# Later token chunks of a GeGLU feed-forward: the gate and up corrections as seven block products with sums outside PSUM

## The chip, the core and the metric

One NeuronCore of a Trainium2 chip runs the whole program. Its engines work side by side, each on its own queue in order: TensorE (PE; its weight loads are shown as PEld), VectorE (DVE), ScalarE (ACT), GpSimd (POOL) and SyncE (SP), which issues most DMAs. Matrix products go to PSUM, eight banks of 128 x 512 float32; operands come from SBUF. Engines wait for each other by semaphores. The metric is the time of one execution on the device in microseconds (us), the median of several.

## The reference

One transformer block in float32 with 2048 tokens of width 640: attention in a window of 256, then a feed-forward of width 1536 with a gate.

```python
def _B_ref(x, w_gate, w_up, w_down):
    return (_gelu(x @ w_gate) * (x @ w_up)) @ w_down

x = A_x
h = x + _A_ref(_layernorm(x, axis=-1), A_wqkv, A_wo)
h2 = h + _B_ref(_layernorm(h, axis=-1), B_w_gate, B_w_up, B_w_down)
return h2
```

## The kernel before

TensorE works in float16 at a quarter of the price of float32, so each float32 operand is split into two float16 parts, a high one and a low one (`wh`, `wl` of a weight; `hh`, `hl` of the normalised tokens). A product is then three matmuls: high x high, high x low, low x high (`parts`). Weights are scaled by a power of two first, so that the low parts don't vanish; `WE` is that exponent, `ffk` holds the factors that undo it.

The feed-forward runs over four chunks of 512 tokens (`NCH`, `CB` blocks of 128) and, in each, over three groups of 512 features (`FG`) of four tiles of 128 (`FT`). For a chunk `c` and a group `fg`, `gate_up` makes for each tile `ft` the gate product and the up product: 5 slices of the width (`KC`) x 3 parts = 15 matmuls of 512 columns into one of two `mm` banks each. `gate_out` then runs beside it: ScalarE takes the gate bank through GELU into `gel`, VectorE multiplies the up bank onto it (`gel`), ScalarE writes the high part `ah`, VectorE the low part `al`. `down` multiplies `ah`, `al` by the down weights: eight groups (4 token blocks x 2 halves of the width) of 12 matmuls of 320 columns, each into an `mm` bank, which VectorE adds to the rows `ht` (`down_out`); that addition frees the bank. Rows that are complete leave for `out_dram`; the next chunk but one then loads its rows into their place (`chunk_lane`), and `norm_lane` normalises them: VectorE's statistics (`BN_STATS`), `lxn`, ScalarE's high part `sph`, VectorE's low part `spl`, and DMA transposes into `hTh`, `hTl`.

The order of instructions on each engine is not written out: the program is a set of lanes (Python generators), and a planner (`Clock`, and the loop at the end of `block_kernel`) keeps a running estimate of each engine's time and takes the next step of the first lane that can start. What it decides while the program is built is fixed on the chip. TensorE's own lane in the feed-forward is `feed_forward`: `gate_up` of a group, then `down` of the group before. Chunk 0 begins while the attention still runs; `split_lane` makes the parts of the weights as they arrive, the high part on ScalarE, the low one on VectorE (`low`; its other branch, ScalarE and GpSimd, is there but unused). All instructions are recorded through one helper, so the profile gives line 190 to all.

```python
for w in (wg_, wu_):
    wh, wl = w.hl
    ps = yield from products(KC, lambda k: parts((wh[:, k, fs], wl[:, k, fs]),
                                                 (hh[:, k, :], hl[:, k, :])),
                             lambda k: k in w.have)
```

Of the kernel before, what the change touches and what calls it, by code (L numbers as in the profile page):

```python
# [11 lines left out]
F32 = mybir.dt.float32  # L12
# [4 lines left out]
ALU = mybir.AluOpType  # L17
# [20 lines left out]


WE = 14  # L40
XE = 10
QE = -23
VE = -20
ME = 15
UE = -43


def _pow2(e):
    return float(2.0 ** e)
# [192 lines left out]
def block_kernel(ctx: ExitStack, tc: tile.TileContext, x, wqkv, wo, wg, wu, wd, out):  # L242
# [21 lines left out]
    def done(name):  # L264
        opened[name] -= 1
# [64 lines left out]
    class Weight:  # L330
# [3 lines left out]
        hl = None  # L334
        loaded = scaled = known = sliced = down = begun = False

        def __init__(self, src, shape, col):
            self.src, self.shape, self.col = src, shape, col
            self.have = set()
            self.raw = {}  # L340

# [24 lines left out]
        def scale(self, lane, tp="tp"):  # L366
            n = self.shape[0]
            am = nc.tile(lnp, [P, 8], F32, "am" + lane, 2 if lane == "0" else 1)
            nc.vector.memset(am[:, n:n + 1], _pow2(-100))
            for i in range(n):  # L370
                if self.hl:

                    yield on("scalar", self.raw[0, i])
                    nc.scalar.activation(self.hl[0][:, i, :], self.raw[0, i], AF.Abs,
                                         accum_out=am[:, i:i + 1])
                    continue
                yield on("vector", when=lambda: (0, i) in self.raw)
# [9 lines left out]
            nc.vector.tensor_scalar(dg, ident, am[:, 7:8], _pow2(-WE), op0=ALU.mult, op1=ALU.mult)  # L387
# [16 lines left out]
            nc.vector.tensor_scalar(pc, pc, _pow2(WE), None, op0=ALU.mult)  # L404
            self.known = True

        def room(self, pool):
# [31 lines left out]
        W[n] = Weight(wqkv[g], [KC, D], C_Q + g)  # L439
    W["o", 0] = Weight(wo, [KC, D], C_WO)  # L440
    for g in range(FG):
        W["g", g] = Weight(wg[g], [KC, 512], C_G + g)
        W["u", g] = Weight(wu[g], [KC, 512], C_U + g)
        W["d", g] = Weight(wd[g], [FT, D], C_D + g)


# [97 lines left out]

    def ff_scales(fg):
        gs, us = C_G + fg, C_U + fg
        nc.vector.tensor_scalar(ffk[:, fg, 0:1], pw[:, gs:gs + 1], _pow2(-WE - XE), None,
                                op0=ALU.mult)
        nc.vector.tensor_scalar(ffk[:, fg, 4:5], pw[:, gs:gs + 1], 0.5 * _pow2(-WE - XE), None,
                                op0=ALU.mult)  # L550
        nc.vector.tensor_scalar(ffk[:, fg, 1:2], sw[:, gs:gs + 1], _pow2(UE), None, op0=ALU.mult)
        nc.vector.tensor_tensor(ffk[:, fg, 3:4], pw[:, us:us + 1], pw[:, gs:gs + 1], op=ALU.mult)

    def ff_scales_down(fg):
        ds_ = C_D + fg
        nc.vector.tensor_scalar(ffk[:, fg, 2:3], ffk[:, fg, 3:4], pw[:, ds_:ds_ + 1],
                                _pow2(-WE - XE - UE - WE - WE), op0=ALU.mult, op1=ALU.mult)


    attn = ExitStack()  # L560
# [480 lines left out]
    def gate_out(c, fg, ft, pss):  # L1041

        pool = ffpools[(c * FG + fg) % 2]
        ah, al = ga[c, fg]
        gel = nc.tile(pool, [P, CB * P], F32, "gel", 2)
# [12 lines left out]
    def gate_up(c, fg):  # L1058
        pool = ffpools[(c * FG + fg) % 2]
        wg_, wu_ = W["g", fg], W["u", fg]  # L1060
        yield pe(when=lambda: wg_.hl and chunk[c] == CB)
        hh, hl = hT[c]
        ah = nc.tile(pool, [P, FT, CB * P], F16, "ah")
        al = nc.tile(pool, [P, FT, CB * P], F16, "al")
        ga[c, fg] = ah, al
        for ft in range(FT):
            fs = slice(ft * P, (ft + 1) * P)
            yield pe(when=lambda: opened["gel"] < 2)
            pss = []
            for w in (wg_, wu_):  # L1070
                yield pe(when=lambda: w.hl)
# [8 lines left out]
                yield  # L1080

    def down(c, fg):
        w = W["d", fg]
# [36 lines left out]
            hts[c].append(ht)  # L1120

    def chunk_lane(c):
        yield ("sync",), need(when=lambda: c == 0 or W["u", 2].ready
                              and (c < 2 or chunk["out", c - 2] == CB), eng="sync")
        load_h(c, ffpools[c % 2], CB)
        if c:
            hT[c] = tuple(nc.tile(ffp, [P, KC, CB * P], F16, n, 2) for n in ("hTh", "hTl"))
            side.extend((LATE, norm_lane(c, bs, n)) for bs, n in (((0, 2), "h"), ((1, 3), "i")))

    def norm_lane(c, bs, lane):  # L1130
        for b in bs:
            yield from layernorm(hts[c][b], lane, *hpart(c, b),
                                 xn=lambda: nc.tile(ffp, [P, D], F32, "lxn", 2), dma=True)
            chunk[c] += 1

    def first_norm_lane():

# [118 lines left out]

    def feed_forward():
        order = [(c, fg) for c in range(NCH) for fg in range(FG)]
        prev = None
        for c, fg in order[1:]:  # L1260
            yield from gate_up(c, fg)
            if prev:
                yield from down(*prev)
            prev = (c, fg)
        yield from down(*prev)

# [140 lines left out]
```

## Time and profile before

| | before |
|---|---|
| median of 3 runs | 1069.77 us (1068.78 to 1072.12) |
| span of the profiled execution, first to last instruction | 1063.8 us |
| PE busy | 1038.2 us, 98% of the span |
| DVE busy | 659.2 us, 62% |
| ACT busy | 461.0 us, 43% |
| POOL busy | 183.4 us, 17% |
| mean granted TensorE clock | 0.995 |

The profiled execution has no time of its own but its span; the median of the runs is 5.97 us above that span. The attention takes some 620 us of it, and from about 697 us on TensorE works on chunks 1 to 3 of the feed-forward. In the profile's rows a group reads: line, engine, operation, output <- inputs with their shapes, count, duration (mean, or min/median/max, in ns). A timeline row begins with start and duration in us; in brackets stands the idle time of the engine just before, and what ended it.

### The profile page before, as it was taken

How to read it: one execution, taken by the hardware profiler on the slowest of the kernel's cores; microseconds unless marked ns; L12 is line 12 of the kernel's file. 1: busy time of each engine (PE TensorE's matmuls, PEld its weight loads, DVE VectorE, ACT ScalarE, POOL GpSimd, SP SyncE). 2: the span in 40 equal slices, each digit the busy share in tenths (PEclk: the TensorE clock that was granted, in tenths of full speed). 3: DMA queues.
4: the chain of work that ended last, by engine and by line, in shares of the span. 5: the costliest groups of instructions: out<-in, count | busy, mean ns of one | idle time of the engine just before them, and what ended most of it. 6: DMA issues, size and time to landing. Idle time of an engine off the chain costs nothing.

```text
span 1063.8 us, 25769 instructions
## 1 busy us (share of the span) xinstructions
PE 1038.2 (98%) x10486; PEld 649.8 (61%) x10486; DVE 659.2 (62%) x1966; ACT 461.0 (43%) x890; POOL 183.4 (17%) x297
## 2 busy tenths in 40 slices
PE   7999899999999999999999999999999999999998
PEld 7977466766776666676655664555545545545546
DVE  5678899997778877677789469823622262322223
ACT  5521666665666656567666835310211120111010
POOL 5000223232233223323332400000000000000000
PEclk9999999999999999999999999999999999999999
DMA  7562444543141321414321034202300040001001
GB/s 285 136 156 69 123 139 106 154 114 78 44 110 57 87 67 52 101 52 94 106 104 51 27 121 153 45 6 99 50 1 1 28 107 15 1 1 50 1 1 50
DMA packets 79382, 80.89 MB, mean 76 GB/s; under 512 B 22240, under 2 KB 58336, under 8 KB 78304
## 3 DMA queue, kind: packets, MB, share of 16 engines
q1 hardware_dynamic: 56160, 68.50, 22.7%
q10 hardware_dynamic: 23104, 10.75, 3.8%
q8 instruction: 82, 1.34, 0.5%
q14 instruction: 36, 0.29, 0.1%
HBM read 54.07 MB, written 20.97 MB: 71 GB/s over the span
## 4 chain that ended last, share of the span: by engine, by line
PE 86%; DVE 8%; DMA 2%; issue 2%; ACT 1%; POOL 0%; SPq 0%; DVEq 0%; ACTq 0%; POOLq 0%
PE mm L190 65%; PE pv L190 9%; PE ra L190 4%; PE rb L190 4%; PE tp L190 4%; DVE junk L190 3%; DMA qk<-qks 1%; DMA kT<-qk 1%; ACT pt L190 1%; DVE gu L190 0%; DVE am L190 0%; DVE lstx L190 0%; DVE w3l L190 0%; DVE ht L190 0%; DMA xt<-in_x_dram 0%
## 5 line engine op out<-in xcount | busy, mean ns | idle before, releaser
L190 POOL TENSOR_SCALAR_AFFINE_SELECT pt<-pt 128x512 f32<-128x512 f32 x240 | 151.0, 651 | 332.6 <-ACT pt L190 327.5
L190 DVE CUSTOM_DVE_ANT_0 junk<-ra,mask 128x384 bf16<-128x384 f32 (+2 forms) x266 | 141.3, 531 | 42.4 <-PE ra L190 21.8
L190 ACT ACTIVATE pt<-rb,esc 128x384 f32<-128x384 f32 (+2 forms) x248 | 131.4, 581 | 67.2 <-PE rb L190 47.1
L190 DVE CUSTOM_DVE_ANT_0 junk<-rb,mask 128x384 bf16<-128x384 f32 (+2 forms) x246 | 130.1, 529 | 42.8 <-PE rb L190 25.7
L190 ACT ACTIVATE pt<-ra,esc 128x384 f32<-128x384 f32 (+2 forms) x232 | 121.8, 577 | 77.0 <-PE ra L190 67.1
L190 DVE SCALAR_TENSOR_TENSOR gel<-mm,ffk,gel 128x512 f32<-128x512 f32 x48 | 36.0, 749 | 146.3 <-PE mm L190 146.3
L190 ACT ACTIVATE gel<-mm,ffk 128x512 f32<-128x512 f32 x48 | 33.0, 688 | 190.6 <-PE mm L190 190.6
L190 PE MATMUL pv<-pt,v 128*21 128x128 f32 x2880 | 105.6, 277 | 0.8 <-ACT oT L190 0.6
L190 DVE SCALAR_TENSOR_TENSOR ht<-mm,ffk,ht 128x320 f32<-128x320 f32 x96 | 52.8, 550 | 80.5 <-PE mm L190 80.3
L190 PEld LDWEIGHTS <-ah 128*128 128x128 f16 x768 | 75.1, 98 | 31.2 <-issue 0.8
L190 ACT CAST ah<-gel 128x512 f16<-128x512 f32 x48 | 29.7, 618 | 128.7 <-DVE gel L190 128.7
L190 PEld LDWEIGHTS pv<-pt,v 128*21 128x21 f32 x2880 | 69.0, 101 | 16.0 <-issue 2.2
L190 PEld LDWEIGHTS <-gu 128*128 128x128 f16 x480 | 45.7, 98 | 53.7 <-issue 1.9
L190 PE MATMUL mm<-hTh,gu 128*128 128x512 f16 x240 | 71.9, 379 | 0.0
L190 PEld LDWEIGHTS <-kT 62*128 62x128 f16 x1440 | 58.3, 95 | 21.4 <-issue 10.9
L190 PEld LDWEIGHTS <-qT 60*128 60x128 f16 x640 | 24.8, 93 | 63.2 <-issue 59.8
L190 PE MATMUL mm<-xl,w1h 128*128 128x256 f16 x200 | 54.7, 273 | 0.0
L190 PE MATMUL mm<-xl,w0h 128*128 128x256 f16 x200 | 54.6, 273 | 0.0
L190 PE MATMUL mm<-xh,w1l 128*128 128x256 f16 x200 | 54.6, 273 | 0.0
L190 PE MATMUL mm<-xh,w1h 128*128 128x256 f16 x200 | 54.6, 273 | 0.0
L190 PE MATMUL mm<-xh,w0l 128*128 128x256 f16 x200 | 54.6, 273 | 0.0
L190 PE MATMUL mm<-xh,w0h 128*128 128x256 f16 x200 | 54.6, 273 | 0.0
(219 smaller groups left out, 2341.7 us busy)
## 6 DMA issues: line engine op xcount, KB each, us to landing
qk<-qks ACTq DMA_DIRECT2D x64, 128.0 KB
qT<-qk SPq DMA_DIRECT2D x48, 160.0 KB
kT<-qk SPq DMA_DIRECT2D x48, 160.0 KB
ht<-in_x_dram SPq DMA_DIRECT2D x16, 320.0 KB
h_dram<-ht SPq DMA_DIRECT2D x16, 320.0 KB
ht<-h_dram SPq DMA_DIRECT2D x16, 320.0 KB
out_dram<-ht SPq DMA_DIRECT2D x15, 320.0 KB
xt<-in_x_dram SPq DMA_DIRECT2D x13, 320.0 KB
```

What stands on the lines that cost most here:

```text
L190: r = real(*args, **kw)
```

## The change

For chunks 1 to 3, gate and up products of a tile are no longer made one by one. The 512 tokens are cut in two halves, 1 and 2, and the corrections of gate (g) and up (u) are taken as one 2 x 2 block product: rows are the gate and up weights, columns the token halves, and the index summed over is (low, high). Eight block products stood there: for each of g and u and each half, low weight x high token and high weight x low token. They become seven, by the known scheme with sums of blocks ahead of and behind the products (Winograd's form of Strassen's). Two of the seven run on plain operands, the others on sums: four sums of weights per tile (`weight_sums`: two on GpSimd, two on VectorE, each 128 x 640) and four of tokens per chunk (`token_sums`: two on each engine, each 128 x 1280). High x high is multiplied as before.

Per tile TensorE now runs 10 matmuls of 512 columns and 35 of 256 (`quad`), into four PSUM banks (`tp`, `ra`, `pv`, `rb`, which the attention has left). `quad_out` adds the blocks up: ScalarE copies `tp` and `pv` to SBUF (`r0` or `gelt`, `r1`), GpSimd makes four additions of 128 x 256 in these, VectorE adds the results to the `ra` and `rb` banks; GELU, product, `ah` and `al` follow as before. `down` of the group before is no longer a run of eight groups: `fill` puts two of them behind each quad.

Around it: the exponent of gate and up weights is 13 in place of 14 (the sums need room); the first two low parts of each later weight go by ScalarE and GpSimd (`split(..., 2)`); the next chunk's rows may be planned once the last gate weight, not the last up weight, is ready; chunk 2 uses chunk 0's `h0h`, `h0l` for its transposed rows; the token sums use the buffers `wst` of the loaded weights.

```diff
+    def quad(c, fg, ft, fill):
...
+        h1, h2 = hh[:, :, :CW], hh[:, :, CW:]
+        l1, l2 = hl[:, :, :CW], hl[:, :, CW:]
+        yield pe(slots=["tp"], when=lambda: c in TS and (c, fg, ft) in WS)
+        t, s = TS[c], WS.pop((c, fg, ft))
...
+        xs = bank("tp")
+        span(xs[:, :CW], gl, h1)
+        yield pe(s[:, 1], t[:, 1])
+        span(xs[:, CW:], s[:, 1], t[:, 1])
...
+        gs = bank("ra")
+        span(gs, gh, hh, stop=False)
+        yield pe(l1)
+        span(gs[:, :CW], gh, l1, start=False, stop=False)
+        yield pe(s[:, 3])
+        span(gs[:, CW:], s[:, 3], l2, start=False)
+        yield pe(s[:, 2], t[:, 2], slots=["pv"])
+        xs = bank("pv")
+        span(xs[:, :CW], s[:, 2], t[:, 2])
+        yield pe(s[:, 0], t[:, 0])
+        span(xs[:, CW:], s[:, 0], t[:, 0])
...
+        us = bank("rb")
+        span(us, uh, hh, stop=False)
+        yield pe(t[:, 3])
+        span(us[:, :CW], uh, t[:, 3], start=False)
+        part.append(us)
+        yield from fill()
...
+    def quad_out(c, fg, ft, part):
...
+            nc.scalar.copy(r[k], part[k])
+            done(("tp", "pv")[k])
+            for o, i in (((0, 1), (0, 0)),) if k == 0 else (((1, 0), (0, 1)), ((0, 1), (1, 1)),
+                                                            ((1, 1), (1, 0))):
+                a, b = (r[m][:, CW * n:CW * n + CW] for m, n in (o, i))
+                yield on("gpsimd", a, b)
+                nc.gpsimd.tensor_tensor(a, a, b, op=ALU.add)
...
+        nc.vector.tensor_tensor(gel, gs, r[0], op=ALU.add)
...
+        nc.scalar.activation(gel, gel, AF.Gelu_apprx_tanh, scale=ffk[:, fg, 0:1])
...
+        nc.vector.tensor_tensor(r[1], part[3], r[1], op=ALU.add)
...
+        nc.vector.scalar_tensor_tensor(gel, r[1], ffk[:, fg, 1:2], gel, op0=ALU.mult,
+                                       op1=ALU.mult)
...
+    def token_sums(c):
...
+        nc.gpsimd.tensor_tensor(t[:, 0], h2, h1, op=ALU.subtract)
...
+        nc.vector.scalar_tensor_tensor(t[:, 1], t[:, 0], -_pow2(-TE), l2, op0=ALU.mult,
+                                       op1=ALU.add)
...
+        nc.gpsimd.tensor_tensor(t[:, 3], l1, t[:, 1], op=ALU.subtract)
...
+        nc.vector.scalar_tensor_tensor(t[:, 2], l2, _pow2(TE), h2, op0=ALU.mult,
+                                       op1=ALU.subtract)
...
+    def weight_sums(c, fg, ft):
...
+        nc.gpsimd.tensor_tensor(t[:, 2], gl, ul, op=ALU.subtract)
...
+        nc.vector.scalar_tensor_tensor(t[:, 0], uh, _pow2(-TE), ul, op0=ALU.mult, op1=ALU.add)
...
+        nc.vector.scalar_tensor_tensor(t[:, 1], t[:, 2], -_pow2(TE), uh, op0=ALU.mult,
+                                       op1=ALU.add)
...
+        nc.gpsimd.tensor_tensor(t[:, 3], gh, t[:, 1], op=ALU.subtract)
...
-            yield from w.split(ffpools[k])
+            yield from w.split(ffpools[k], 2)
...
+        def sums_lane():
+            for i, q in enumerate(quads):
+                yield on("gpsimd", when=lambda: pos["quads"] >= i - 1 and W["d", 2].ready)
+                yield from weight_sums(*q)
...
+            def fill():
+                for _ in range(2):
+                    for y in groups:
+                        if y is None:
+                            break
+                        yield y
...
+            for ft in range(FT):
+                yield from quad(c, fg, ft, fill)
+                pos["quads"] += 1
```

How the order moves, first VectorE at the end of chunk 0, where the eight down groups of its second feature group stand ahead of chunk 1. `ht` rows free `mm` banks; `ws` and `wst` are sums of weights and of tokens. Before:

```order
L190 TENSOR_TENSOR spl<-lxn,sph 128x640
L190 TENSOR_TENSOR al<-gel,ah 128x512
L190 SCALAR_TENSOR_TENSOR ht<-mm,ffk,ht 128x320 x3
L190 TENSOR_TENSOR spl<-lxn,sph 128x640
L190 SCALAR_TENSOR_TENSOR ht<-mm,ffk,ht 128x320 x5
L190 SCALAR_TENSOR_TENSOR gel<-mm,ffk,gel 128x512
```

And now:

```order
L192 TENSOR_TENSOR spl<-lxn,sph 128x640
L192 SCALAR_TENSOR_TENSOR ht<-mm,ffk,ht 128x320
L192 TENSOR_TENSOR al<-gel,ah 128x512
L192 SCALAR_TENSOR_TENSOR ws<-gu 128x640
L192 SCALAR_TENSOR_TENSOR ht<-mm,ffk,ht 128x320
L192 SCALAR_TENSOR_TENSOR ws<-ws,gu 128x640
L192 SCALAR_TENSOR_TENSOR ht<-mm,ffk,ht 128x320 x2
L192 SCALAR_TENSOR_TENSOR wst<-wst,hTl 128x5x256
L192 SCALAR_TENSOR_TENSOR ht<-mm,ffk,ht 128x320
L192 SCALAR_TENSOR_TENSOR wst<-hTl,hTh 128x5x256
L192 SCALAR_TENSOR_TENSOR ht<-mm,ffk,ht 128x320 x3
```

The bank-freeing rows, which stood almost in one run, now alternate with sums.

Second VectorE ahead of chunk 2, behind the last `spl` but one of that chunk's rows. Before:

```order
L190 SCALAR_TENSOR_TENSOR gel<-mm,ffk,gel 128x512
L190 SCALAR_TENSOR_TENSOR ht<-mm,ffk,ht 128x320
L190 TENSOR_TENSOR spl<-lxn,sph 128x640
L190 TENSOR_TENSOR al<-gel,ah 128x512
L190 SCALAR_TENSOR_TENSOR ht<-mm,ffk,ht 128x320 x7
```

Now, from the last `spl` of these rows on (`r` and `gelt` are the copies of the banks):

```order
L192 TENSOR_TENSOR spl<-lxn,sph 128x640
L192 SCALAR_TENSOR_TENSOR gel<-r_13043,ffk,gel 128x512
L192 TENSOR_TENSOR al<-gel,ah 128x512
L192 SCALAR_TENSOR_TENSOR ht<-mm,ffk,ht 128x320
L192 TENSOR_TENSOR gel<-ra,r_13114 128x512
L192 SCALAR_TENSOR_TENSOR ws<-w9h,w9l 128x640
L192 SCALAR_TENSOR_TENSOR wst<-wst,h0l 128x5x256
L192 TENSOR_TENSOR r_13151<-rb,r_13151 128x512
L192 SCALAR_TENSOR_TENSOR ht<-mm,ffk,ht 128x320
L192 SCALAR_TENSOR_TENSOR ws<-ws,w9h 128x640
L192 SCALAR_TENSOR_TENSOR gel<-r_13151,ffk,gel 128x512
L192 SCALAR_TENSOR_TENSOR wst<-h0l,h0h 128x5x256
```

A token sum stands ahead of the additions that free `rb` and `mm`.

Third GpSimd at the same place, where before only the two one-column operations of each normalised block stood (`lyh`, `lyi`):

```order
L192 TENSOR_TENSOR ws<-w6h,ws 128x640
L192 TENSOR_TENSOR r_13114<-r_13114 128x256
L192 TENSOR_TENSOR r_13151<-r_13151,r_13114 128x256
L192 TENSOR_TENSOR r_13114<-r_13114,r_13151 128x256
L192 TENSOR_TENSOR wst<-h0h 128x5x256
L192 TENSOR_TENSOR r_13151<-r_13151 128x256
L192 TENSOR_TENSOR ws<-w6l,w9l 128x640
```

The token sum stands between the additions of one tile.

More of the change, by code (lines that the diff above doesn't have):

```diff
@@ L40 @@
 WE = 14
+GE = 13
 XE = 10
@@ L44 @@
 ME = 15
-UE = -43
+UE = -41
+TE = 10
 def _pow2(e):
@@ L403, in scale @@
             yield on("vector", pc)
-            nc.vector.tensor_scalar(pc, pc, _pow2(WE), None, op0=ALU.mult)
+            nc.vector.tensor_scalar(pc, pc, _pow2(self.e), None, op0=ALU.mult)
             self.known = True
@@ L441, in block_kernel @@
     for g in range(FG):
-        W["g", g] = Weight(wg[g], [KC, 512], C_G + g)
-        W["u", g] = Weight(wu[g], [KC, 512], C_U + g)
+        W["g", g] = Weight(wg[g], [KC, 512], C_G + g, GE)
+        W["u", g] = Weight(wu[g], [KC, 512], C_U + g, GE)
         W["d", g] = Weight(wd[g], [FT, D], C_D + g)
@@ L546, in ff_scales @@
         gs, us = C_G + fg, C_U + fg
-        nc.vector.tensor_scalar(ffk[:, fg, 0:1], pw[:, gs:gs + 1], _pow2(-WE - XE), None,
+        nc.vector.tensor_scalar(ffk[:, fg, 0:1], pw[:, gs:gs + 1], _pow2(-GE - XE), None,
                                 op0=ALU.mult)
-        nc.vector.tensor_scalar(ffk[:, fg, 4:5], pw[:, gs:gs + 1], 0.5 * _pow2(-WE - XE), None,
+        nc.vector.tensor_scalar(ffk[:, fg, 4:5], pw[:, gs:gs + 1], 0.5 * _pow2(-GE - XE), None,
                                 op0=ALU.mult)
@@ L1044, in gate_out @@
         ah, al = ga[c, fg]
-        gel = nc.tile(pool, [P, CB * P], F32, "gel", 2)
+        gel = nc.tile(ffpools[0], [P, CB * P], F32, "gel", 2)
         yield from gelu(gel, pss[0], fg, pool, (c, fg) == (0, 0))
@@ L1080, in gate_up, with span @@
                 yield
+    def span(o, l, r, start=True, stop=True):
+        n = l.shape[1]
+        for k in range(n):
+            nc.tensor.matmul(o, l[:, k], r[:, k], start=start and k == 0, stop=stop and k == n - 1)
+            pos["dense"] += r[:, k].free_size() // 2
+    def quad(c, fg, ft, fill):
+        fs = slice(ft * P, (ft + 1) * P)
+        (gh, gl), (uh, ul) = (tuple(t[:, :, fs] for t in W[k, fg].hl) for k in "gu")
+        hh, hl = hT[c]
+        h1, h2 = hh[:, :, :CW], hh[:, :, CW:]
+        l1, l2 = hl[:, :, :CW], hl[:, :, CW:]
+        yield pe(slots=["tp"], when=lambda: c in TS and (c, fg, ft) in WS)
+        t, s = TS[c], WS.pop((c, fg, ft))
+        part = []
+        tasks.append(quad_out(c, fg, ft, part))
+        xs = bank("tp")
+        span(xs[:, :CW], gl, h1)
+        yield pe(s[:, 1], t[:, 1])
+        span(xs[:, CW:], s[:, 1], t[:, 1])
+        part.append(xs)
+        yield pe(slots=["ra"])
+        gs = bank("ra")
[9 more added lines that the diff above has]
+        span(xs[:, CW:], s[:, 0], t[:, 0])
+        part.extend((xs, gs))
+        yield pe(slots=["rb"])
+        us = bank("rb")
[4 more added lines that the diff above has]
+        yield from fill()
@@ new lines, in quad_out @@
+    def quad_out(c, fg, ft, part):
+        pool = ffpools[(c * FG + fg) % 2]
+        ah, al = ga[c, fg]
+        r = []
+        names = "gelt" if ft % 2 else "r0", "r1"
+        for k, n in enumerate(names):
+            yield on("scalar", when=lambda: len(part) > k and not opened[n])
+            opened[n] += 1
+            r.append(nc.tile(ffpools[0] if n == "gelt" else ffp, [P, 512], F32, n))
+            yield on("scalar", part[k])
+            nc.scalar.copy(r[k], part[k])
[5 more added lines that the diff above has]
+                nc.gpsimd.tensor_tensor(a, a, b, op=ALU.add)
+        gs = part[2]
+        yield on("vector", gs, r[0], when=lambda: opened["gel"] < 2)
+        opened["gel"] += 1
+        gel = nc.tile(ffpools[0], [P, CB * P], F32, "gel", 2)
+        nc.vector.tensor_tensor(gel, gs, r[0], op=ALU.add)
+        done("ra")
+        opened[names[0]] -= 1
+        yield on("scalar", gel)
+        nc.scalar.activation(gel, gel, AF.Gelu_apprx_tanh, scale=ffk[:, fg, 0:1])
+        yield on("vector", r[1], when=lambda: len(part) > 3)
+        yield on("vector", part[3], r[1])
+        nc.vector.tensor_tensor(r[1], part[3], r[1], op=ALU.add)
+        done("rb")
+        yield on("vector", gel, r[1])
+        nc.vector.scalar_tensor_tensor(gel, r[1], ffk[:, fg, 1:2], gel, op0=ALU.mult,
+                                       op1=ALU.mult)
+        opened[names[1]] -= 1
+        yield on("scalar", gel)
+        nc.scalar.copy(ah[:, ft, :], gel)
+        yield on("vector", ah[:, ft, :])
+        nc.vector.tensor_tensor(al[:, ft, :], gel, ah[:, ft, :], op=ALU.subtract)
+        opened["gel"] -= 1
+        pos["act", c, fg] += 1
@@ L1126, in chunk_lane @@
         if c:
-            hT[c] = tuple(nc.tile(ffp, [P, KC, CB * P], F16, n, 2) for n in ("hTh", "hTl"))
+            hT[c] = hT[0] if c == 2 else tuple(nc.tile(ffp, [P, KC, CB * P], F16, n)
+                                               for n in ("hTh", "hTl"))
             side.extend((LATE, norm_lane(c, bs, n)) for bs, n in (((0, 2), "h"), ((1, 3), "i")))
@@ L1258, in feed_forward @@
         order = [(c, fg) for c in range(NCH) for fg in range(FG)]
+        quads = [(c, fg, ft) for c, fg in order[FG:] for ft in range(FT)]
+        def sums_lane():
+            for i, q in enumerate(quads):
+                yield on("gpsimd", when=lambda: pos["quads"] >= i - 1 and W["d", 2].ready)
+                yield from weight_sums(*q)
+        side.append((LATE, sums_lane()))
         prev = None
-        for c, fg in order[1:]:
+        for c, fg in order[1:FG]:
             yield from gate_up(c, fg)
@@ L1263, in feed_forward @@
                 yield from down(*prev)
+            prev = (c, fg)
+        for c, fg in order[FG:]:
+            groups = down(*prev)
+            def fill():
[4 more added lines that the diff above has]
+                        yield y
+            pool = ffpools[(c * FG + fg) % 2]
+            ga[c, fg] = tuple(nc.tile(pool, [P, FT, CB * P], F16, n) for n in ("ah", "al"))
+            for ft in range(FT):
+                yield from quad(c, fg, ft, fill)
+                pos["quads"] += 1
             prev = (c, fg)
```

32 lines of the change are left out of this document (27 added, 5 removed).

## The prediction

> **What bounds the kernel now.** I read the chain of waits first, then the busy time of the engines in the stage that the change touches. The chain (start, length, what):
>
> ```profile
> by line: PE mm L190 99.0%; PE tp L190 0.2%; DVE ht L190 0.1%; issue 0.0%
> 670.16 390.28 PE mm L190 x2199
> 1060.46 0.55 DVE ht L190
> ```
>
> From 670 us to the end it is one unbroken run of matmuls. The windows view says the same of 700 to 1060 us:
>
> ```profile
> core 0: us, PE busy (x) PEld busy (x) DVE busy (x) ACT busy (x) POOL busy (x), PEclk, DMA share, GB/s
> 700.00:1060.00 360.00, 360.00 (x2025) 197.94 (x2024) 117.02 (x223) 52.38 (x80) 5.10 (x8) 1.00 0.10 29
> ```
>
> TensorE is busy for all 360 us at full clock; VectorE a third of it; GpSimd hardly at all. So a matmul less is worth its issue interval, and work put on VectorE or GpSimd is free until TensorE has to wait for it. A matmul's recorded length (0.38 us) overlaps the next one; the interval is read from the starts:
>
> ```profile
> 715.11 0.38 PE L190 MATMUL mm<-hTl,gu 128*128 128x512 f16 x1
> 722.23 0.38 PE L190 MATMUL mm<-hTl,gu 128*128 128x512 f16 x1
> 722.66 0.30 PE L190 MATMUL mm<-w12h,ah 128*128 128x320 f16 x1
> 724.29 0.30 PE L190 MATMUL mm<-w12h,ah 128*128 128x320 f16 x1
> 31.96 0.27 PE L190 MATMUL mm<-xh,w1h 128*128 128x256 f16 x1
> 33.82 0.27 PE L190 MATMUL mm<-xh,w1l 128*128 128x256 f16 x1
> ```
>
> 33 steps between the first two: 0.2158 us for 512 columns. 12 steps between the next two: 0.1358 us for 320. 17 between the last two, each with a weight load of its own: 0.1094 us for 256.
>
> **What is removed on TensorE.** Of chunks 1 to 3, each of the 36 feature tiles (3 chunks, 3 groups, 4 tiles) now takes 30 matmuls of 512 columns. A `quad` takes 10 of 512 and 35 of 256. That is 20 x 0.2158 - 35 x 0.1094 = 0.487 us less each, 36 x 0.487 = **17.5 us**. With its two groups of the down product (24 of 320 columns, 3.26 us) a quad lasts 2.16 + 3.83 + 3.26 = 9.25 us, where 9.73 us stand now.
>
> **What is added, and where it meets.** Per quad VectorE gets two operations on 128x640 (`ws`) and two adds out of PSUM; GpSimd two adds of 640 and four of 256 elements; ScalarE two copies. The prices of the operations that are there:
>
> ```profile
> L190 DVE TENSOR_TENSOR spl<-lxn,sph x12: 809/818/821, 672.5 to 880.7; 128x640 f16<-128x640 f32 x12
> L190 DVE SCALAR_TENSOR_TENSOR gel<-mm,ffk,gel x48: 734/751/753, 553.8 to 1034.5; 128x512 f32<-128x512 f32 x48
> L190 ACT CAST ah<-gel x48: 603/618/669, 555.2 to 1035.2; 128x512 f16<-128x512 f32 x48
> L190 ACT ACTIVATE gel<-mm,ffk x48: 665/687/725, 548.6 to 1031.2; 128x512 f32<-128x512 f32 x48
> L190 DVE SCALAR_TENSOR_TENSOR ht<-mm,ffk,ht x37: 543/551/553, 690.4 to 852.7; 128x320 f32<-128x320 f32 x37
> ```
>
> VectorE: 2 x 0.82 + 3 x 0.75 + 0.69 (`al`) + 2 x 0.55 = 5.7 us of 9.25. ScalarE: 3 x 0.62 + 0.69 = 2.6 us. Neither is full. But VectorE and GpSimd get in each other's way, as the trace shows at 555 us:
>
> ```profile
> L190 POOL TENSOR_SCALAR_AFFINE_SELECT pt<-pt x240: 628/634/1217, 111.5 to 612.1; 128x512 f32<-128x512 f32 x120
> L190 DVE TENSOR_TENSOR al<-gel,ah x48: 673/691/1114, 556.6 to 1035.9; 128x512 f16<-128x512 f32 x48
> L190 DVE SCALAR_TENSOR_TENSOR w10l<-wst,sw,w10h x4: 877/878/1049, 555.7 to 562.6; 128x640 f16<-128x640 f32 x4
> L190 DVE CUSTOM_DVE_ANT_0 junk<-ra,mask x266: 272/558/560, 63.2 to 582.0; 128x384 bf16<-128x384 f32 x117, 128x128 bf16<-128x128 f32 x8, 128x256 bf16<-128x256 f32 x8
> 555.41 1.80 POOL L190 TENSOR_SCALAR_AFFINE_SELECT pt<-pt 128x512 f32<-128x512 f32 x2 [3.36 <-ACT pt L190]
> 555.67 1.05 DVE L190 SCALAR_TENSOR_TENSOR w10l<-wst,sw,w10h 128x640 f16<-128x640 f32 x1
> 556.65 1.11 DVE L190 TENSOR_TENSOR al<-gel,ah 128x512 f16<-128x512 f32 x1
> ```
>
> Two selects, `w10l` and `al` overlap there, and three of the four are stretched: the second select to 1.217 us (0.583 over its median), `w10l` by 0.17, `al` by 0.42. Each begins to work about 0.15 us before the other's recorded end: they take turns at something. `junk`, with one operand in PSUM and one in SBUF, never exceeds 0.560 us in 266, under many selects. So VectorE operations with two SBUF operands and GpSimd operations that read SBUF exclude each other; I call it the port. In the change it is wanted by `ws`, the final `gel` product, `al`, `spl`, the token sums, and every GpSimd add.
>
> The price of a GpSimd add does not stand in the trace. Below: the select, one input, 0.634 us / 512 = 1.24 ns per element. Above: twice that for two inputs, 2.48. I take **2.1**, nearer the upper, since every add reads twice what a select reads: 0.54 us for 256, 1.34 for 640, 2.69 for a token sum of 1280.
>
> *Steady quads.* GpSimd 2 x 1.34 + 4 x 0.54 = 4.84, VectorE 2 x 0.82 + 0.75 + 0.69 = 3.08, less ten hand-overs of 0.15: the port is taken 6.4 us of 9.25 (4.4 at the low price, 7.3 at the high). It fits: no wait of TensorE. Its banks are covered too: `tp` and `pv`, single, are asked for again only after some 8 us of other matmuls. At the end two down groups (3.26 us) cover the chain of the last tile, 0.75 + 0.75 + 0.62 + 0.69 = 2.8 us; that is the cost if the cover goes.
>
> *Entry into chunk 1.* Now the last transposed rows are issued here, and the first matmul on them follows 6.7 us later:
>
> ```profile
> 690.12 1.29 SPq L190 DMA_TRANSPOSE hTl<-spl  x1
> L190 PE MATMUL mm<-hTh,gu x240: 379/379/379, 696.8 to 956.1; 128*128 128x512 f16 x120
> ```
>
> In between TensorE runs eight down groups of 1.63 us with two `mm` banks, each freed by a VectorE `ht`. The new order puts two `ws` pairs and the two VectorE token sums between those `ht` rows, and GpSimd's two token sums fall there too. Whenever a 2.69 us sum has the port, a VectorE operation waits for it, works (0.82), and only then `ht` (0.55) frees a bank; TensorE has about half a group (0.8) left: 2.69 + 0.82 + 0.55 - 0.8 = 3.25 us, twice, 6.5. The later weights' first two low parts now go over GpSimd, and TensorE already waits once for such a part there:
>
> ```profile
> L190 PEld LDWEIGHTS <-w9l 128*128 128x128 f16 x80 | 7.8, 98 | 10.7 <-DVE w9l L190 1.9
> ```
>
> I add 1.0 (0 to 1.5). Entry: **7.5 us** (4.3 at the low price with nothing added, 9.0 at the high).
>
> *Sums of chunks 2 and 3.* They stand in the last two or three quads ahead of each chunk. In two of these the port is asked for 2 x 6.4 (quads) + 2 x 2.69 + 2 x 1.49 (VectorE's token sums, two `spl` lengths less 0.15) - 0.6 = 7.8 (sums) + 1.3 (two `spl`) = 21.9 us, where 18.5 are there: 3.4 us short. A fixed order leaves holes besides, since `ws` goes GpSimd, VectorE, VectorE, GpSimd and `gel` waits for GpSimd's adds: 1.2 us a quad (0 to 2.4, by a whole 640 add and its neighbour). Each: **5.9 us** (0 at the low price, 8.6 at the high). While a VectorE operation waits, `ht` and the add that frees `rb` stand behind it, so TensorE pays.
>
> Sum: -17.5 + 7.5 + 2 x 5.9 = **+1.8 us**. The profiled span is 1063.8 us, so 1065.6; the median run, 1069.8, is 6.0 above the span, and I keep that: **1071.6 us**. Low price: -17.5 + 4.3 = -13.2, 1056.6. High price: -17.5 + 9.0 + 17.2 = +8.7, 1078.5.
>
> Two rules of the Trainium skill bear on this. GPSIMD Engine Reference, section 3.1, has 4497 ns for an add of 2048 elements, 2.2 ns each; by it the sum would be some 1.7 us higher, 1073.3. SBUF — State Buffer, section Who interferes with whom, says the port belongs to one engine for a whole instruction; the trace agrees up to 0.63 us (`al`), and for 2.7 us no run here shows it. Were it handed over within an instruction, the entry would cost about 2 and the later sums 3.4 each, 1061.
>
> **Rivals.** *Faster, about 1060.* GpSimd's adds cost little more than a select, and the holes stay small: 1.4 ns per element gives 4.7 at the entry and under 1 at each later chunk, -17.5 + 6.7 = -10.8, 1059. For it: 1.24 ns is the only GpSimd price measured here on wide tiles. Against: two operands.
>
> *Slower, about 1079: VectorE waits for rows with bank-freeing work behind it.* Today it already does, harmlessly:
>
> ```profile
> 740.03 0.89 DVE L190 BATCH_NORM_STATS2 lsth<-ht 128x6 f32<-128x320 f32 x2 [3.58 <-DMA ht<-h_dram]
> 857.07 0.89 DVE L190 BATCH_NORM_STATS2 lsth<-ht 128x6 f32<-128x320 f32 x2 [3.79 <-DMA ht<-h_dram]
> ```
>
> In the change `gel`, `ws` and `ht` queue behind these statistics. If the rows are late again, two times 3.6 us shift the `ws` that TensorE needs in the next quad: +7.2, 1078.8. It decides once the wait exceeds the third of a quad that VectorE has free (3.5 us). Against: the down groups are spread over the quads, so the rows of the chunk before leave earlier.
>
> *Not what it says.* If 35 weight loads (0.098 us recorded, under 0.1094) no longer hide, since `ws` arrives just in time, the 17.5 us shrink: half of them gone gives 1080, all 1089.
>
> **Chances.** Given back at the port: 0.45, own range 1067 to 1077; faster rival 0.30; slower rival 0.20; not what it says 0.05. The range of 8 in 10 reaches from the low price (1056.6) to the high price with one of the rows' waits and more, 1057 to 1086. A measurement tells 0.3%, 3.2 us. Within it lie 0.27 of the first case and 0.02 of the second; faster 0.01 + 0.28; slower 0.17 + 0.20 + 0.05. So faster 0.29, same 0.29, slower 0.42.
>
> **What would show it.** Starts of 256-column matmuls 0.109 us apart, and quads of 9.25 us in the middle of a chunk: the 17.5 us. GpSimd `ws` and `r` groups: mean ns over elements gives the price; 1.3 or 2.5 in place of 2.1 moves the time as above. `al`, `spl` and `ws` on VectorE with maxima of 2 to 3 us against medians of 0.7 to 0.8: the port. TensorE idle before `mm` released by VectorE `ht`, some 7 us ahead of the first quad and 6 ahead of each later chunk, none elsewhere. I am wrong if TensorE waits in every quad, or if those waits are absent.

## The result, and the profile after

| | before | after |
|---|---|---|
| median of 9 runs each | 1069.77 us (1067.53 to 1072.12) | 1077.96 us (1072.39 to 1081.23) |
| ratio, 95% interval | | 1.0081 (1.0060 to 1.0102) |
| span of the profiled execution | 1063.8 us | 1074.7 us |
| granted clock | 0.995 | 0.987 |

The change is slower, by 8.2 us in the medians. The forecast was 1071.6 us, in a range of 1057 to 1086, with slower the likeliest side. The profiled spans differ by 10.9 us. Matched matmul by matmul, the changed kernel is already 2.1 us behind at 629 us, ahead of the first wait listed below (2.8 at 116 us, 1.3 at 540 us), so the feed-forward from there on adds 8.8; that agrees with the medians.

The page of the changed kernel, busy times and the engines of the chain of waits:

```profile
PE 1029.9 (96%) x11026; PEld 704.6 (66%) x11026; DVE 795.5 (74%) x2102; ACT 511.2 (48%) x976; POOL 445.4 (41%) x533
PE 65%; DVE 16%; POOL 8%; issue 6%; ACT 2%; DMA 2%; SPq 0%; DVEq 0%; ACTq 0%; POOLq 0%
```

The window 700 to 1060 us, with the columns that the prediction shows:

```profile
700.00:1060.00 360.00, 348.40 (x2551) 250.86 (x2550) 249.66 (x368) 92.61 (x152) 240.19 (x226) 0.98 0.09 27
```

Before, 360 of these 360 us were matmuls at full clock. Now VectorE works 250 us there (117 before) and GpSimd 240 (5 before). TensorE is idle for 11.6 us, and the clock is down to 0.98, which is some 7 us of lost work in 360, a part of it while TensorE stood still. What TensorE waited for from 618 us to the end (total, times, longest, in us):

```profile
PE mm L192 <- ACT ah L192: 9.9, 2, 5.0
PE mm L192 <- DVE ht L192: 6.2, 6, 3.2
PE mm L192 <- POOL w9l L192: 1.1, 2, 0.6
PE pv L192 <- ACT r L192: 0.2, 1, 0.2
```

Between the waits the change does what it says. Starts of a quad's first five matmuls, and of the five that follow its first ten:

```profile
783.34 0.71 PE L192 MATMUL tp<-hTh,w6l 128*128 128x256 f16 x5
...
784.44 1.24 PE L192 MATMUL ra<-hTh,w6h 128*128 128x512 f16 x5
```

Ten matmuls of 256 columns in 1.10 us. The quads of the first two groups of chunk 1 start at 709.43, 718.67, 727.91 and so on to 783.34: eight steps of 9.24 us each.

The waits and what follows them, from the distances of the starts, beside the terms of the prediction. They are some 0.16 us longer each than in the view above, where idle time begins only at the recorded end of a matmul, which overlaps the next one; and short ones are counted too, so the sum is 21.0 in place of 17.4.

| place | waits, us | lost to half clock, us | predicted, us |
|---|---|---|---|
| low parts of later weights (630 to 668) | 3.4 | 0.1 | 1.0 |
| entry into chunk 1 (690 to 707) | 4.4 | 2.9 | 6.5 |
| third group of chunk 1 and entry into chunk 2 (786 to 826) | 6.5 | 1.4 | 5.9 |
| third group of chunk 2 and entry into chunk 3 (905 to 945) | 6.5 | 1.5 | 5.9 |
| end | 0.2 | 0 | 0 |
| sum | 21.0 | 5.9 | 19.3 |

21.0 + 5.9 - 17.5, less 0.3 of waits that stood in the kernel before, is +9.1, where 8.8 was measured. So the sum of the waits came out near the forecast, in part by luck, as more at the low parts and less at the entry nearly cancel. Three things did not come out: half clock behind the long waits, the price of the low parts, and the place of the two waits of 5 us.

**Prices.** Duration in ns, least/median/most, of GpSimd's and VectorE's groups:

```profile
L192 POOL TENSOR_TENSOR r<-r x54: 715/727/1309, 711.4 to 1055.6; 128x256 f32<-128x256 f32 x54
L192 POOL TENSOR_TENSOR ws<-gu x12: 1395/1400/1981, 683.5 to 965.9; 128x640 f16<-128x640 f16 x12
L192 POOL TENSOR_TENSOR wst<-hTl,wst x2: 2606/2892/3177, 703.3 to 924.1; 128x1280 f16<-128x1280 f16 x2
...
L192 DVE TENSOR_TENSOR gel<-ra,r x18: 691/692/693, 716.3 to 1046.3; 128x512 f32<-128x512 f32 x18
L192 DVE TENSOR_TENSOR al<-gel,ah x37: 677/681/1642, 692.8 to 1058.9; 128x512 f16<-128x512 f32 x37
L192 DVE SCALAR_TENSOR_TENSOR gel<-r,ffk,gel x36: 731/806/3091, 718.1 to 1057.4; 128x512 f32<-128x512 f32 x36
L192 DVE SCALAR_TENSOR_TENSOR ws<-gu x11: 809/812/3215, 694.2 to 967.7; 128x640 f16<-128x640 f16 x11
```

GpSimd: 0.72 us for 256, 1.40 for 640, 2.61 for 1280; from 640 to 1280 that is 1.88 ns per element, with 0.19 us ahead of them. The long ones cost what was forecast (1.34 and 2.69); the adds of 256, four in each quad, are a third dearer than the 0.54 forecast. VectorE's operations with two SBUF operands are stretched to 1.6 to 3.2 us; the add with one operand in PSUM (`ra`) never leaves 0.69.

**The entry.** VectorE and GpSimd where TensorE waits 3.15 us for `ht`:

```profile
694.18 3.21 DVE L192 SCALAR_TENSOR_TENSOR ws<-gu 128x640 f16<-128x640 f16 x1
697.32 0.54 DVE L192 SCALAR_TENSOR_TENSOR ht<-mm,ffk,ht 128x320 f32<-128x320 f32 x1
...
693.67 3.04 POOL L192 TENSOR_TENSOR wst<-hTh 128x1280 f16<-128x1280 f16 x1
...
697.91 0.43 PE L192 MATMUL mm<-w11h,ah 128*128 128x320 f16 x1 [3.15 <-DVE ht L192]
```

This is the collision of the prediction: a token sum holds the port, `ws` waits for all that is left of it, and `ht`, which frees the bank, stands behind. By the Trainium skill (SBUF — State Buffer, section Who interferes with whom) the port belongs to one engine for a whole instruction; before, the trace bore that out to 0.63 us, now it does to 2.4 (`ws`, 3.21 less its 0.81).

**The waits of 5 us.** Not at a token sum, as forecast, but ahead of them (GpSimd begins those of chunk 2 at 798.0). A chain that is on time, and the late one:

```profile
725.57 0.69 DVE L192 TENSOR_TENSOR gel<-ra,gelt 128x512 f32<-128x512 f32 x1 [4.09 <-POOL gelt L192]
...
788.44 0.69 DVE L192 TENSOR_TENSOR gel<-ra,gelt 128x512 f32<-128x512 f32 x1 [1.42 <-POOL gelt L192]
...
789.50 1.75 DVE L192 SCALAR_TENSOR_TENSOR ws<-w9h,w9l 128x640 f16<-128x640 f16 x1
...
791.91 0.68 DVE L192 TENSOR_TENSOR r<-rb,r 128x512 f32<-128x512 f32 x1
...
792.96 1.17 DVE L192 TENSOR_TENSOR spl<-lxn,sph 128x640 f16<-128x640 f32 x1
794.06 1.21 DVE L192 SCALAR_TENSOR_TENSOR gel<-r,ffk,gel 128x512 f32<-128x512 f32 x1
...
795.97 0.45 PE L192 MATMUL mm<-w11h,ah 128*128 128x320 f16 x1 [4.95 <-ACT ah L192]
```

The first `gel` comes 6.9 us after its quad began (718.67). The second belongs to the quad that began at 774.11: 14.3 us, so the chain had fallen behind by 7 us already. It is the last tile of its group, and `down` needs all four. From 754.7 us on VectorE also normalises the next chunk. An estimate from the rows: a quad takes the port 4 x 0.72 + 2 x 1.40 on GpSimd, 2 x 0.81 + 0.74 + 0.68 on VectorE, less ten hand-overs of 0.15: 7.2 of 9.24 us, where 6.4 was forecast. Four quads make 28.9; the four blocks of a chunk add 4 x (0.61 `lxn` + 0.81 `spl`) = 5.7 and four small GpSimd operations of 0.55, one for each block. That is 36.8 of 37.0 us: full, by this estimate, with every hole a loss.

**Half clock.** Windows around two of the waits (columns as above; PEclk is the third from the end):

```profile
694.50:698.00 3.50, 0.35 (x3) 0.15 (x2) 3.50 (x3) 0.00 (x0) 2.21 (x1) 0.82 0.02 6
698.00:703.40 5.40, 5.40 (x21) 2.95 (x21) 3.00 (x4) 0.00 (x0) 1.45 (x2) 0.50 0.00 0
...
790.70:796.00 5.30, 0.35 (x4) 0.03 (x2) 4.62 (x7) 0.70 (x2) 2.65 (x2) 0.98 0.29 58
796.00:799.20 3.20, 3.19 (x12) 1.57 (x13) 2.30 (x4) 0.78 (x2) 2.59 (x3) 0.51 0.05 9
```

TensorE is busy throughout 698.0 to 703.4 and 796.0 to 799.2, with half as many matmuls as the time would hold. Such a stretch follows each of the three long waits, and none of the short ones.

### The profile page after: what moved, and what is told of

It is laid out like the page before. It is cut to its first block, busy times and chain, and to the rows that moved or that the text cites. A ratio compares the mean times of both kernels' runs of the same rounds, so it can differ in the third digit from the quotient of the medians.

```text
span 1074.7 us, 27473 instructions
## 1 busy us (share of the span) xinstructions
PE 1029.9 (96%) x11026; PEld 704.6 (66%) x11026; DVE 795.5 (74%) x2102; ACT 511.2 (48%) x976; POOL 445.4 (41%) x533
## 4 chain that ended last, share of the span: by engine, by line
PE 65%; DVE 16%; POOL 8%; issue 6%; ACT 2%; DMA 2%; SPq 0%; DVEq 0%; ACTq 0%; POOLq 0%
PE mm L192 34%; PE pv L192 11%; PE ra L192 8%; PE rb L192 7%; PE tp L192 6%; DVE junk L192 4%; POOL r L192 3%; POOL ws L192 2%; DVE gel L192 1%; DVE ws L192 1%; DMA qk<-qks 1%; POOL wst L192 1%; DVE am L192 1%; POOL gelt L192 1%; ACT pt L192 1%
## 5 line engine op out<-in xcount | busy, mean ns | idle before, releaser
L192 DVE CUSTOM_DVE_ANT_0 junk<-ra,mask 128x384 bf16<-128x384 f32 (+2 forms) x260 | 137.9, 530 | 40.5 <-PE ra L192 20.6
L192 DVE CUSTOM_DVE_ANT_0 junk<-rb,mask 128x384 bf16<-128x384 f32 (+2 forms) x252 | 133.4, 529 | 43.7 <-PE rb L192 26.1
L192 ACT ACTIVATE pt<-ra,esc 128x384 f32<-128x384 f32 (+2 forms) x240 | 126.3, 578 | 75.2 <-PE ra L192 66.2
L192 ACT ACTIVATE pt<-rb,esc 128x384 f32<-128x384 f32 (+2 forms) x240 | 127.1, 581 | 70.4 <-PE rb L192 49.5
L192 ACT ACTIVATE gel<-gel,ffk 128x512 f32<-128x512 f32 x36 | 26.0, 722 | 108.3 <-DVE gel L192 108.3
L192 PEld LDWEIGHTS <-ws 128*128 128x128 f16 x720 | 70.4, 98 | 8.6 <-issue 0.4
L192 PEld LDWEIGHTS <-gu 128*128 128x128 f16 x420 | 39.9, 98 | 28.5 <-issue 1.4
L192 PE MATMUL mm<-w11h,ah 128*128 128x320 f16 x128 | 41.0, 320 | 14.6 <-ACT ah L192 9.9
```

Source lines behind the costliest of these rows:

```text
L192: r = real(*args, **kw)
```

## The experiments

The theory after the result: the port is full while the next chunk is normalised beside the quads, VectorE falls behind, TensorE waits 5 us, and the clock halves behind such a wait. The rivals: the token sums are too much (the prediction), VectorE has too much to do, the latency of GpSimd's adds, slow stretches of another origin. All ratios are to the kernel before, run on the same chip; the change itself stands at 1.0081. The planner orders VectorE's work anew in most of these kernels (the run with filled waits keeps the order), so a part of a difference can lie in the order and is not separated from the rest.

| run | median, us | ratio, 95% interval |
|---|---|---|
| no later token sums | 1079.13 | 1.0088 (1.0060 to 1.0116) |
| no later normalisation | 1060.67 | 0.9952 (0.9926 to 0.9978) |
| adds from PSUM on VectorE | 1064.30 | 0.9959 (0.9939 to 0.9980) |
| the same, with idle adds on GpSimd | 1077.66 | 1.0084 (1.0054 to 1.0113) |
| waits filled with matmuls | 1075.46 | 1.0064 (1.0040 to 1.0087) |
| waits made in the kernel before | 1113.32 | one run, beside 1068.33 |
| short token sums | 1074.49 | 1.0064 (1.0041 to 1.0087) |
| low parts on VectorE | 1072.44 | 1.0035 (1.0017 to 1.0053) |
| adds from PSUM and short sums | 1055.96 | 0.9889 (0.9863 to 0.9915) |

**Which work makes the 5 us waits?** Two kernels, each without one part.

```diff
     def token_sums(c):
...
+        if c > 1:
+            yield on("vector", l2)
+            TS[c] = TS[1]
+            return
```

> The token sums of chunks 2 and 3 are left out (the sums of chunk 1 are used again, so the rows of chunks 2 and 3 come out wrong); everything else of the change stays. Theory: the two 5.1 us waits of TensorE, one ahead of chunk 2 and one ahead of chunk 3, come from the normalisation of the next chunk, which fills the port together with the quads, before any token sum stands there. Both waits stay at 4 to 5.5 us with their stretches of half clock; only the waits of 0.71 and 0.45 us go, and the holds of the sums: 1074 to 1077 us. Rival (step 7 of the prediction): the token sums are what is too much; both 5.1 us waits and their slow stretches go, 2 x (5.1 + 0.35 + 1.4) + 1.2 = 15 us less, about 1063.

```diff
     def norm_lane(c, bs, lane):
...
+            if c == 1:
+                yield from layernorm(...)
+            else:
+                yield on("vector", hts[c][b])
```

> The normalisation of chunks 2 and 3 is left out (their rows are still loaded and added to, but the rows of chunks 0 and 1 are multiplied in place of theirs); the quads, the weight sums and the token sums of all chunks stay. Theory: the 5.1 us waits come from the normalisation of the next chunk beside the quads, so both go with the slow stretches behind them, and the 0.7 and 0.45 us too; up to 1.2 us may stand where the token sums now fall: 12 to 15 us less, 1063 to 1066 us; the entry stays. Rival (the quads alone fill the port, and any small addition tips them): the 5.1 us waits shrink to 2 to 3 us, 1070 to 1073 us.

TensorE's longest sort of wait from 690 us on, first without the sums, then without the normalisation:

```profile
PE mm L192 <- ACT ah L192: 9.9, 2, 5.0
```

```profile
PE mm L192 <- DVE ht L192: 3.7, 2, 3.2
```

Without the sums both 5.0 us waits for `ah` stand as they were, and only the 0.71 and 0.45 us go. The time cannot be told from the change's; it did not even fall to the 1074 to 1077 expected, and 1063 is excluded. Without the normalisation both are gone: 1064.6 us by the ratio. The prediction's cause falls; the normalisation is what brings these waits.

**The port, or VectorE's load, or the adds' latency?** The same sums, with each add taking one operand from PSUM:

```diff
-            nc.scalar.copy(r[k], part[k])
...
-                nc.gpsimd.tensor_tensor(a, a, b, op=ALU.add)
...
+            if k == 0:
+                nc.scalar.copy(a1, x1)
+                nc.vector.tensor_tensor(a2, x2, a1, op=ALU.add)
+            else:
+                nc.vector.tensor_tensor(a1, x1, b, op=ALU.add)
+                nc.vector.tensor_tensor(b, x2, b, op=ALU.add)
+                nc.vector.tensor_tensor(a2, x2, a1, op=ALU.add)
```

> The four GpSimd adds of 256 elements in each quad (0.72 us each) become four VectorE adds that take one operand from PSUM; one of ScalarE's two copies goes, the other is halved. The same sums are computed. VectorE gets some 1.4 us more per quad, and GpSimd's claim on the port falls by 2.9 us of 9.24. Theory (the port): no TensorE wait above 0.7 us in chunks 1 to 3, no stretch of half clock there; the entry into chunk 1 keeps its wait of 3.3 us. 2 x (5.1 + 0.35 + 1.4) + 1.2 + 0.6 = 15.5 us less: about 1062. Rival (VectorE simply has too much work): VectorE is busy some 50 us longer, the waits grow, above 1080.

And that kernel with four adds per quad on a tile (`ghost`) that nothing reads:

```diff
+            for _ in range(1 + 2 * k):
...
+                yield on("gpsimd", g)
+                nc.gpsimd.tensor_tensor(g[:, :CW], g[:, CW:2 * CW], g[:, D - CW:], op=ALU.add)
```

> As the run with the adds from PSUM, but GpSimd also does four adds of 256 elements per quad on a tile that nothing else uses: nobody waits for their result. Theory (the port): the waits come back, each 3 us or more, although no result depends on GpSimd any more: 1074 to 1082. Rival (the latency of GpSimd's adds in the chain from PSUM to gel, not the port): as without them, about 1062.

With the adds from PSUM, VectorE's new adds:

```profile
L192 DVE TENSOR_TENSOR r<-pv,r x72: 365/415/426, 718.8 to 1045.0; 128x256 f32<-128x256 f32 x72
```

its page:

```profile
PE 1028.3 (97%) x11026; PEld 704.2 (66%) x11026; DVE 829.3 (78%) x2246; ACT 484.3 (45%) x940; POOL 323.2 (30%) x389
```

and TensorE's two longest sorts of wait from 690 us on:

```profile
PE mm L192 <- DVE ht L192: 5.0, 3, 3.2
PE ra L192 <- POOL ws L192: 0.6, 2, 0.3
```

With the idle adds, its page, the same group of VectorE and GpSimd's idle adds, then TensorE's three longest sorts of wait:

```profile
PE 1023.6 (96%) x11026; PEld 701.2 (65%) x11026; DVE 857.0 (80%) x2246; ACT 484.0 (45%) x940; POOL 448.9 (42%) x534
L192 DVE TENSOR_TENSOR r<-pv,r x72: 369/415/426, 711.4 to 1051.2; 128x256 f32<-128x256 f32 x72
L192 POOL TENSOR_TENSOR wsl<-wsl x144: 717/727/1970, 704.1 to 1044.6; 128x256 f32<-128x256 f32 x144
```

```profile
PE mm L192 <- DVE ht L192: 6.8, 5, 3.2
PE ra L192 <- POOL ws L192: 5.4, 2, 2.7
PE mm L192 <- DVE al L192: 4.3, 2, 2.2
```

With the adds from PSUM both 5 us waits are gone, and behind the entry, which keeps 3.3 and 1.8 us, no wait is longer than 0.5 us. VectorE works 34 us more than in the change, and by the ratios the kernel is 13 us faster: its load is not the cause. GpSimd's adds alone, with no result that anyone waits for, bring 13.4 us back: the latency of the adds in the chain is not what costs them. The same 2246 VectorE instructions now take 857.0 us in place of 829.3, while the adds from PSUM take 0.415 us in both kernels, so an operand in PSUM keeps VectorE out of the way. The waits came back around 787 to 809 and 906 to 928 us, near the old ones, but shorter than expected, 0.6 to 2.9 us. Of them, the 5.4 us for GpSimd's own `ws` may come from its queue as much as from the port; the others name VectorE.

**Does the half clock follow from standing still?** In the kernel before, nine waits of growing length:

```diff
+    def hold(n):
...
+        nc.scalar.copy(t[:, :P], one)
+        for _ in range(n):
+            nc.scalar.copy(t, t)
+        nc.scalar.copy(u, t[:, :P])
+        nc.tensor.matmul(two, u, ident16, start=True, stop=True)
```

> The kernel before, with nine waits made for TensorE, one in each group of features of chunks 1 to 3: between two matmuls whose results are dropped stands a chain of ScalarE copies of 512 elements (about 0.6 us each), 0, 1, 2, 3, 4, 5, 6, 8 and 10 of them and two short ones. Waits of about 1 to 7.5 us, 34 us in sum. Theory (the half clock follows from TensorE standing still for most of some 3.4 us): none after the waits under 2 us, always a stretch of 2.5 to 5.5 us at half clock after those over 5 us, and sometimes after those of 2.5 to 4 us; each costs 1.3 to 2.9 us on top of its wait; 1069 + 34 + 5 x 2 = 1113 us. Rival (the slow stretches have another cause): the clock stays at 1.00 throughout, 1104 us.

Idle time ahead of the released matmul for the third, fourth and ninth wait:

```profile
792.36 0.23 PE L190 MATMUL ra<-ident,wsl 128*128 128x128 f16 x1 [1.99 <-ACT wsl L190]
834.22 0.23 PE L190 MATMUL ra<-ident,wsl 128*128 128x128 f16 x1 [2.64 <-ACT wsl L190]
1063.80 0.29 PE L190 MATMUL ra<-ident,wsl 128*128 128x128 f16 x1 [7.18 <-ACT wsl L190]
```

The windows that follow them:

```profile
792.40:796.60 4.20, 4.20 (x21) 1.96 (x22) 0.67 (x1) 0.49 (x1) 0.00 (x0) 1.00 0.00 0
834.20:838.50 4.30, 4.28 (x14) 1.64 (x15) 0.00 (x0) 0.55 (x1) 0.00 (x0) 0.62 0.00 0
1063.80:1067.30 3.50, 3.50 (x10) 1.29 (x11) 0.00 (x0) 0.53 (x1) 0.00 (x0) 0.50 0.00 0
```

After 0.69, 1.34 and 1.99 us the clock stays at 1.00; after each of the six longer ones, 2.64 to 7.18 us, the clock of the next 3 to 4.5 us is 0.50 to 0.63 in the mean. Length times what is missing of the clock gives 1.5 to 2.1 us for each, 10 in sum; with 31.5 us of waits that makes most of the 45 us by which the run was longer. The length does not decide alone: with the idle adds, waits of up to 3.2 us were followed by full clock (a window of that kernel):

```profile
696.90:703.30 6.40, 6.35 (x47) 4.59 (x47) 5.71 (x6) 0.00 (x0) 3.90 (x2) 1.00 0.00 1
```

The Trainium skill (TensorE: Matmul & The Clock Gate, Part 1: The HAM clock gate) has a free-running window of 3.4 us: TensorE goes to half clock after an idle window, and back after a busy one. That the same 3.2 us wait halves the clock in one execution and not in another fits a window that runs free; that 2.64 us was enough does not fit a window that must be wholly idle. The starts show the window: behind the 2.64 us wait, which ends at 834.2 us, matmuls of 512 columns still start 0.22 us apart until 835.2, then 0.43 apart until 838.6, that is for 3.4 us. Of the 3.4 us ahead of 835.2, TensorE had worked about 1.

What the stretches cost in the change itself, with dropped matmuls in place of the waits:

```diff
+        if (c, fg, ft) in ((1, 2, 0), (2, 2, 0)):
+            busy("mm", 24, gh, hh)
         yield from fill()
...
+                if (c, fg, b, nh) == (0, 1, 1, 1):
+                    busy("ra", 15, W["g", 2].hl[0][:, :, :P], hT[0][0])
```

> The change as it is, with matmuls whose results are dropped at the three places where TensorE waits longest: 15 of 512 columns (3.2 us) ahead of the fourth group of the down product at the entry into chunk 1, and 24 (5.2 us) ahead of the first group in the third group of features of chunks 1 and 2. The other engines' orders are unchanged. Theory (the half clock follows from TensorE standing still): the matmuls fill the waits, the granted clock stays at 1.0, and the three slow stretches go: 2.9 + 1.4 + 1.5 = 5.8 us less, 1071 to 1073. Rival (the slow stretches have another cause): they stay, and the time is that of the change or a little longer, 1078.

The same stretch as above:

```profile
698.00:703.40 5.40, 5.40 (x39) 3.63 (x38) 4.71 (x8) 0.00 (x0) 2.28 (x2) 1.00 0.00 2
```

The clock is whole, 39 matmuls where 21 stood, yet of 5.8 us only some 2 came (1.8 by the ratios, 2.5 by the medians; the intervals overlap). The rest turned into waits for `ht`: at 705.0 us TensorE now stands 1.80 us (0.61 before), and around the entries into chunks 2 and 3 1.92 and 1.91 (0.71 and 0.45). A TensorE at half speed had given VectorE time to catch up. So, by this trace, the half clock is for the larger part not a cost of its own but the form in which VectorE's lateness was paid.

**The entry.** Shorter holds, and the low parts put back:

```diff
+        for k in range(KC):
+            yield on("gpsimd", h1[:, k], h2[:, k])
+            nc.gpsimd.tensor_tensor(t[:, 0, k], h2[:, k], h1[:, k], op=ALU.subtract)
```

> GpSimd's two token sums of each chunk are made in five pieces of 256 elements (about 0.73 us each) in place of one of 1280 (2.6 us): the same sums, some 1 us more of GpSimd and of the port in each, but no long hold. Theory (whoever meets a hold waits for the rest of that one instruction, so at the entry it is the length of the holds that counts): the waits of 3.3 and 0.6 us at the entry fall to about 1 us in sum, and the slow stretch behind them goes; the 5.1 us waits ahead of chunks 2 and 3 stay, since they do not come from the token sums; -3 to -5 there, up to +2.4 at each of the two later sums, which end later: 1072 to 1078 us. Rival (the amount of port time counts): the entry's waits grow by about 2 us, 1080.

```diff
-            yield from w.split(ffpools[k], 2)
+            yield from w.split(ffpools[k])
```

> The first two low parts of each later weight go back from GpSimd to VectorE (as before the change); the rest of the change stays. Theory: the waits of 1.6 us for w9l go; at the entry VectorE has fewer ht in a row with the sums, the 3.3 us wait goes, but the token sums are late in their place and TensorE waits up to 4.9 us for wst ahead of the first quad; the 5.1 us waits stay. 1 to 4 us less: 1074 to 1077 us. Rival (the low parts on GpSimd carry the entry): all of the entry's waits go, 1.6 + 3.9 + 2.9 = 8.4 us less, 1070.

A piece of the short sums, and three of VectorE's low parts in the change; then TensorE's two longest sorts of wait from 618 us on with the low parts on VectorE:

```profile
628.17 3.87 DVE L192 SCALAR_TENSOR_TENSOR w5l<-wst,sw,w5h 128x512 f16<-128x512 f32 x3
...
L192 POOL TENSOR_TENSOR wst<-hTh x10: 668/674/1250, 694.5 to 917.6; 128x256 f16<-128x256 f16 x10
```

```profile
PE mm L192 <- ACT ah L192: 9.9, 2, 5.0
PE tp L192 <- DVE wst L192: 3.2, 1, 3.2
```

In five pieces a sum takes 5 x 0.67 = 3.4 us of GpSimd in place of 2.6, and the wait at the entry is 1.38 us in place of 3.31, the 0.61 gone, the clock whole: it is the length of one hold that counts there, not the amount. The time fell by only 1.8 us by the ratios, which is not clear of the noise; the half clock behind the two 5 us waits lasts longer in this trace (5.2 and 4.4 us, where it was 3.2 and 3.7). With the low parts back, the waits for `w9l` and for the `ht` at 630 us go; a new one of 3.2 us for a late token sum (`wst`) takes the place of the entry's. 5 us less in all, somewhat more than expected.

**Both together.** The adds from PSUM and the short sums.

> The adds of each quad from PSUM on VectorE, and the token sums in five pieces on GpSimd. All results are computed. Theory: the 5.1 us waits are gone (by the adds) and the entry's 3.3 and 1.8 us too (by the pieces), with the slow stretch behind them; 1.6 us for w9l and about 1 us at the entry are left: 3.7 + 1.7 us under the adds alone, about 1059 us, the kernel before times 0.990. Rival (the pieces help as little as the port time they take): 1064 us.

All of TensorE's waits from 618 us on:

```profile
PE mm L192 <- DVE ht L192: 3.5, 5, 1.6
PE mm L192 <- POOL w9l L192: 1.1, 2, 0.6
PE tp L192 <- DVE dg L192: 0.2, 1, 0.2
```

4.8 us of waits in place of 17.4, no slow stretch, and a time 1.1% below the kernel before (0.9 to 1.4%): 12 of the 17.5 us that seven products save are kept.

## Why the prediction was right, and where it was not

- *Seven products save 17.5 us.* Right: quads of 9.24 us where 9.25 was worked out, so the 35 weight loads stayed hidden.
- *The port gives it back.* Right as a mechanism, and shown by the idle adds: VectorE operations with two SBUF operands and GpSimd wait for each other, an operand in PSUM takes no part. The list of the prediction lacked `lxn`. The faster rival, cheap adds, fell with the price of 0.72 us. Of the slower one nothing is seen: no statistics of VectorE's wait for rows.
- *Steady quads.* Right that TensorE does not wait in them; the port's share was set too low, 6.4 us against 7.2, since the adds of 256 cost 0.72 and not 0.54.
- *Entry.* The collision is the one described; 4.4 us of waits against 6.5. The second one cost 0.6 because TensorE ran at half clock just then; at full clock it is 1.8.
- *Low parts on GpSimd.* Mis-sized: 3.4 us against 1.0. The term looked at `w9l` alone. At 628 to 632 us two such parts on GpSimd (3.06 us) stretch three low parts of VectorE from 2.07 us (before the change) to 3.87, and the `ht` behind them comes 1.8 us late. The run with the parts put back shows it.
- *"Sums of chunks 2 and 3. They stand in the last two or three quads ahead of each chunk."* This step failed. The size was near, 6.5 us against 5.9 (its own rows give 5.8), but that is luck, for the reason is another: the quads and the normalisation fill the port a group earlier, and taking the sums away leaves the waits as they are. The step counted `spl` in the two quads with the sums, and did not add up the port over the four quads in which the whole normalisation falls.
- *What was missing.* Half clock behind waits of 2.6 us and more: 5.9 us in the trace, about 2 of them net. With 2.4 more for the low parts and 0.6 at each later chunk, less 2.1 at the entry, the terms differ by 7 us; the time was 6.4 above the forecast. The side, slower, was forecast at 0.42, and the time lies within the range.

## What to carry to other kernels

Add up a shared resource over the stretch in which all its users meet, not over the steady loop: here the loop had room, and the loop with the next chunk's normalisation had none. Work moved to GpSimd beside a busy VectorE can cost VectorE time as well, and an add with one operand in PSUM on VectorE itself was the cheaper place, at 0.42 us against 0.72. When TensorE stands for 3 us, look at the clock behind the wait, but fill the wait only where nothing late stands after it.

## What the runs showed of the hardware

GpSimd's add of two SBUF operands took 0.67 us for 256 float16 elements and 0.72 for float32, 1.40 for 640 and 2.61 for 1280 float16. VectorE's `lxn`, which reads one SBUF tile and two single columns, was stretched too, from 0.61 us to 1.65 at 764.65 us, under a GpSimd `ws`. Operations on a single element per partition wait for the port as well: VectorE's `lyah` took 1.30 us in place of 0.22, under a GpSimd `ws`:

```profile
761.69 0.22 DVE L192 SCALAR_TENSOR_TENSOR lyah<-lyh,lveh 128x1 f32<-128x1 f32 x1 [1.18 <-POOL lyh L192]
778.25 1.30 DVE L192 SCALAR_TENSOR_TENSOR lyah<-lyh,lveh 128x1 f32<-128x1 f32 x1
```
